# Two units' decay logarithms move behind the phase border, and the residual adds are queued together

## The chip, the cores and the metric

The kernel runs on one core of one Trainium2 chip. The metric is the device time of one launch in microseconds; the kernel before has a median of 293.94 us over 7 runs (291.76 to 295.33). Engine names follow the profile: PE is the matmul engine, ACT the activation engine, DVE the vector engine, POOL the one that also issues the DMAs which cast or accumulate, SP the one that issues plain loads, stores and transposes.

## What is computed

A linear recurrence with a complex decay for each channel, and then a gated feed-forward layer on its output:

```python
mag = np.sqrt(a_re * a_re + a_im * a_im)
scale = np.minimum(mag, 0.999) / (mag + 1e-06)
a_re_n, a_im_n = (a_re * scale, a_im * scale)
for t in range(S):                       # S = 768, B = 4, H = 8, D = 48
    new_re = ar * S_re - ai * S_im       # ar, ai: decay of step t
    new_im = ar * S_im + ai * S_re
    S_re, S_im = (new_re + k[t] v[t]^T, new_im)
    y[t] = q[t] @ S_re
...
ffn_out = (gelu(x @ w_gate) * (x @ w_val)) @ w_out      # x: y as 3072 x 384
out = x + sigmoid(x @ w_res) * ffn_out
```

The decay enters through the logarithm of its magnitude, 0.5 ln(re^2 + im^2), cut at ln 0.999, and its angle, arctan(im / re). Both are summed along time, and the sums turn the recurrence into products of scaled and rotated q and k.

## The kernel before

**Tiling.** A chunk `g` is 256 time steps of one batch with all 8 heads: two tiles (`C = 2`) of 128 rows and 384 columns, together 128x768. There are 12 chunks, ordered so that the four batches' first thirds come first. They are grouped into units: unit 0 is chunk 0, unit 1 chunks 1 and 2, unit 2 chunks 3 and 4, unit 3 chunks 5 and 6, up to unit 6 with chunk 11. Chunks 4 to 11 continue an earlier one (`NEXT`), so they need the state before them and its decay.

**Magnitude and angle of one chunk.** `squares(g)` forms the square of the real part (L213) and of the imaginary part (L224 on DVE for chunks 1 to 4, L227 on ACT otherwise) and adds them on DVE into the tile `lm` (L231). `p1_steps(g)` has three steps: `s0` takes the logarithm of `lm` in place and halves and cuts it on DVE (L239); `s1` and `s2` take a logarithm and an exponent of the real part, which gives its inverse, and multiply the imaginary part with it (L249). `p1_arctan` takes the arctangent. `cs_l` sums `lm` along time by matmuls (L267), and a later step takes E and its inverse Ei from them by exponents. `cs_t` does the same for the angles (L286, L288) and reduces them to one turn (L290, L291, L296); it writes its result over `lm`. `p2_sin` makes cosine and sine (the tile CS). `products` multiplies q by E and k by Ei (L349, L354) and by CS into the padded operands padQ and padK (L361), which from chunk 3 on SP transposes by DMA into QT and KT (L365).

**The decay of the state at a chunk's border** is a product of three factors in turned form, 96 partitions by 8 heads. `decay0(g)` makes the first: the exponent of row 0 of `lm` on ACT (1x384), a write of this row to a scratch line in DRAM, and `turn`, two reads of that line in turned order (L311) into the tile `m1`. `decay2` does the same for two rows of E and Ei. `multiply` forms the product on DVE (L342, L343); `enter_state` applies it to the state (L378) and rounds it (L380) for the attention matmuls.

**Order.** The program is written as a ramp (chunks 0 to 4) and then, for each unit u, `phase_x(u)` and `phase_y(u)`. `phase_y(u)` is the gate and value matmuls of unit u (`gv_step`: L575, L579, gelu, L582) with the first half of the next unit's attention and the squares of the unit two ahead; chunk 6 (`HELD`) has its squares in `phase_x(1)`. `phase_x(u)` has the logarithm and exponent work: for the next unit the cumulative sums, exponents and sines, for the unit after it the steps of `p1_steps`, beside the second half of unit u's attention and the output matmuls of unit u-1 (`op_step`, L599, L602). `weave` mixes such streams by written-out fractions of the phase. ACT changes its function table at the borders (L613), and `tab` fixes the order of these table loads and of the functions that need them, but not of copies and squares. A list scheduler then sets each engine's order by program order and by its own model of when an instruction is ready; each engine and each queue works its list in order.

**Queues.** SP has the loads of a, q and k, the output writes (L606) and the transposes. POOL has the loads of v and the weights, the turns, and for each output tile but the last unit's a residual add, an accumulating DMA of x onto the output (L608), which waits for that tile's L606. The output tile `ot` has two buffers, x has eight, `m1` three.

Of the kernel before, what the change touches and what calls it, by code (L numbers as in the profile page):

```python
# [28 lines left out]
def kernel(  # L29
# [34 lines left out]
    I2PI = 1.0 / (2.0 * math.pi)  # L64
    TURN = 3
    LATE0, LATE1 = 0.6, 1.0
    LNMAX = 0.5 * math.log(0.998001)


# [56 lines left out]
    psY = ctx.enter_context(tc.tile_pool(name="psY", bufs=1, space=PSUM))  # L126
    psD = ctx.enter_context(tc.tile_pool(name="psD", bufs=1, space=PSUM))

    T = {}
    order = mybir.DependencyInfo(mybir.DependencyClass.NoSync, mybir.DependencyReason.DATA)  # L130

    def tab(ins):
# [75 lines left out]
    def squares(g):  # L208

        def q0():  # L210
            T["lm", g] = pS.tile([128, W], FP, tag="s", name="lm")
            with paced("gelu"):
                nc.scalar.activation(out=T["lm", g], in_=flat(T["ar", g]), func=AF.Square)  # L213

        def q1():
            if g < 5:
                if g == 0:
                    T["sq"] = hb.tile([128, 4, 2, DM], FP, tag="h2", name="sq0")
                t = T["sq"][:, g % 4].rearrange("p a m -> p (a m)")
            else:  # L220
                t = pE.tile([128, W], FP, tag="E", name="sq")
            T["sq", g] = t
            if g in DVSQ:
                nc.vector.tensor_tensor(out=t, in0=flat(T["ai", g]), in1=flat(T["ai", g]), op=OP.mult)  # L224
            else:
                with paced("gelu"):
                    nc.scalar.activation(out=t, in_=flat(T["ai", g]), func=AF.Square)  # L227

        def q2():
            with paced("gmul"):  # L230
                nc.vector.tensor_tensor(out=T["lm", g], in0=T["lm", g], in1=T["sq", g], op=OP.add)  # L231
        return [q0, q1, q2]

    def p1_steps(g):
# [73 lines left out]
    def turn(nm, g, md, n):  # L308
        m = mp.tile([128, n, H], FP, tag=nm, name=nm)
        for u in range(2):  # L310
            nc.gpsimd.dma_start(out=m[u * D:(u + 1) * D].rearrange("p r h -> p (r h)"),  # L311
                                in_=md.rearrange("r (h d) -> d (r h)", h=H))
        T[nm, g] = m

    def decay0(g):
        if g not in NEXT.values():
            return
        e = T["s", g][0:1, 0:DM]
        act(out=e, in_=T["lm", g][0:1, 0:DM], func=AF.Exp)
        md = dr.tile([1, DM], FP, tag="d1", name="d1")  # L320
        nc.gpsimd.dma_start(out=md, in_=e)
        turn("m1", g, md, 1)

    def decay2(g):
        if g in NEXT.values():
# [13 lines left out]
    def multiply(g):  # L339
        m = T["m2", g]  # L340
        M = mp.tile([128, H], FP, tag="M", name="M")
        nc.vector.tensor_tensor(out=M[0:DD], in0=m[0:DD, 0], in1=m[0:DD, 1], op=OP.mult)  # L342
        nc.vector.tensor_tensor(out=M[0:DD], in0=M[0:DD], in1=T["m1", g][0:DD, 0], op=OP.mult)  # L343
        T["M", g] = M

    def products(g):
# [248 lines left out]
    def op_step(u, jj):  # L595
        h2 = T["h2", u]
        ps = psM.tile([128, DM], FP, tag="mm", padded_shape=[128, 512], name="op")
        for ffi in range(KF):
            nc.tensor.matmul(out=ps, lhsT=h2[:, ffi, jj * 128:(jj + 1) * 128], rhs=wo[:, ffi, :],  # L599
                             start=(ffi == 0), stop=(ffi == KF - 1))  # L600
        ot = ob.tile([128, DM], FP, tag="ot", name="ot")
        nc.vector.scalar_tensor_tensor(out=ot, in0=T["sg", u][:, jj], scalar=1.0, in1=ps, op0=OP.add, op1=OP.mult)  # L602
        t0 = (CHUNK[UNITS[u][0] + jj // C] * C + jj % C) * 128
        if u == NU - 1:
            nc.vector.tensor_tensor(out=ot, in0=ot, in1=T["x", token(u, jj)], op=OP.add)
        nc.sync.dma_start(out=out[t0:t0 + 128, :], in_=ot)  # L606
        if u < NU - 1:
            nc.gpsimd.dma_start(out=out[t0:t0 + 128, :], in_=T["x", token(u, jj)], accum_op=OP.add)  # L608


    def table(nm):
        def f():
# [6 lines left out]
    def token(u, jj):  # L619
        return UNITS[u][0] * C + jj  # L620
# [4 lines left out]
    def call(f, *a):  # L625
        return lambda: f(*a)
# [17 lines left out]
    def phase_x(u):  # L644

        pend = []
        g1 = gs(u + 1)
        p1g = [g for w in range(NU) if P1AT.get(w, w - 2) == u for g in gs(w)]
        now = [g for g in p1g if g in g1]
        ahead = [g for g in p1g if g not in g1]  # L650
        ops = [call(op_step, u - 1, jj) for jj in range(len(gs(u - 1)) * C)]
        att = att_steps(u, 1)
        if not g1:
            weave((0.0, 0.8, att), (0.1, 1.0, ops))
            return

        def csl(g, c):
            pend.append(cs_l(g, c))

        def ex():  # L660
            pend.pop(0)()

        def p1(g):
            return (squares(g) if g == HELD else []) + p1_steps(g) + [call(decay0, g)]
        csls = [call(csl, g, c) for g in g1 for c in range(C)]
        exs = [ex for _ in g1 for _ in range(C)]
        dec = [call(decay2, g) for g in g1]
        cst = [call(cs_t, g, c) for g in g1 for c in range(C)]
        sin = [call(p2_sin, g) for g in g1]
        table("natural_log_exp_and_others")()  # L670
        if now:
            atn = [table("trig_and_small")] + [call(p1_arctan, g) for g in now + ahead]
            pn = zip_steps([p1(g) for g in now])
            weave((0.0, 0.05, pn[:2]), (0.06, 0.1, csls), (0.12, 0.25, pn[2:]), (0.26, 0.4, exs),
                  (0.28, 0.48, zip_steps([p1(g) for g in ahead])),
                  (0.5, 0.5, dec), (0.55, 0.65, atn), (0.62, 0.8, cst), (0.9, 0.95, sin),
                  (0.0, 0.8, att), (0.0, 0.25, ops) if u == 1 else (0.1, 1.0, ops))
            return
        atn = [table("trig_and_small")] + [call(p1_arctan, g) for g in ahead]
        weave((0.0, 0.12, csls), (0.05, 0.5, zip_steps([p1(g) for g in ahead])), (0.12, 0.45, exs),  # L680
              (0.46, 0.46, dec), (0.2, 0.65, cst), (0.7, 0.95, atn + sin), (0.0, 0.8, att), (0.1, 1.0, ops))

    def ramp():

        g0, g1, g2 = gs(0) + gs(1)
        pend = {}

        def csl(g):
            pend[g] = [cs_l(g, c) for c in range(C)]

        def ex(g):
            for f in pend[g]:
                f()
            decay2(g)

        def cst(g):
            for c in range(C):
                cs_t(g, c)
        g3, g4 = gs(2)
        p = {g: p1_steps(g) for g in range(5)}  # L700
        q = {g: squares(g) for g in range(5)}
        pr = products(g0)

        def run(*fs):
            for f in fs:
                f()
        table("natural_log_exp_and_others")()
        run(*q[g0], p[g0][0], p[g0][1])
        csl(g0)
        run(p[g1][1], p[g0][2], q[g1][1], p[g1][2])  # L710
        ex(g0)
        run(p[g2][1], q[g2][1], p[g2][2])
        table("trig_and_small")()
        pr[0]()
        pr[2]()
        for g in (g0, g1, g2):
            if g > g0:
                T["f", g] = flat(T["ar", g])
            p1_arctan(g)
            cst(g)  # L720
            if g == g0:
                run(q[g1][0], q[g1][2], q[g2][0], q[g2][2])
        p2_sin(g0)
        pr[1]()
        pr[3]()
        a0 = attention_first(g0, 0, 0)
        table("natural_log_exp_and_others")()
        run(p[g1][0], p[g2][0])
        run(*a0[:2])
        csl(g1)  # L730
        csl(g2)
        run(*a0[2:4], *q[g3], p[g3][1], p[g3][2])
        ex(g1)
        run(*a0[4:7], *q[g4], p[g4][1])
        ex(g2)
        run(p[g4][2], p[g3][0], p[g4][0], call(decay0, g4), *a0[7:])
        with tc.issue_after(T["row"].ins):
            load_q(2, T["ld", "w", 2])
        table("trig_and_small")()
        p2_sin(g1)  # L740
        p2_sin(g2)
        with tc.issue_after(T["ld", "k", 2].ins):
            load_a(5)
        load_w_out()
        with tc.issue_after(T["ld", "ai", 5].ins):
            load_a(6)
        p1_arctan(g3)
        p1_arctan(g4)
# [34 lines left out]
    for u in range(NU + 1):  # L783
        if u > 0:
            phase_x(u)
        phase_y(u)
        for g in gs(u + 2):
            with paced("turn"):
                load_q(g)
            after_landing(T["k", g], call(load_v, g))  # L790
        while T["a"] < min(NG, gs(u + 1)[-1] + 7 if gs(u + 1) else NG):
            with paced("turn"):
                load_a(T["a"])
# [30 lines left out]
```

## Time and profile before

| | value |
|---|---|
| median of 7 runs | 293.94 us |
| the profiled execution | 294.86 us |
| its span in the trace | 293.1 us |
| granted PE clock, mean | 0.951 |
| POOL waiting for output writes at L608 | 54.1 us, 13 times |
| POOL waiting for row writes before a turn (L311), from a real part's row | 17.0 us, 3 times |
| residual adds | 22 of 192 KB, 4.3 us to landing (median) |
| ACT table loads | 21 of 1.28 us |

The span by stages, each bordered by the first gelu of a unit or the table load that ends its gelus (us busy in the stage, mean granted PE clock):

| stage | us | PE | DVE | ACT | clock |
|---|---|---|---|---|---|
| ramp | 0 to 52.3 | 26.7 | 37.7 | 40.1 | 0.87 |
| y(0) | 52.3 to 68.8 | 15.6 | 13.7 | 11.6 | 0.90 |
| x(1) | 68.8 to 90.6 | 16.1 | 19.8 | 20.1 | 0.99 |
| y(1) | 90.6 to 112.2 | 20.7 | 15.5 | 13.1 | 0.85 |
| x(2) | 112.2 to 132.8 | 19.7 | 17.5 | 18.3 | 1.00 |
| y(2) | 132.8 to 155.7 | 20.3 | 17.9 | 13.5 | 0.93 |
| the rest | 155.7 to 293.1 | 129.4 | 99.6 | 82.8 | 0.99 |

An idle time in a timeline stands in brackets with what ended it. An engine that waits is no loss by itself; it matters when what it does next is waited for.

### The profile page before, as it was taken

How to read it: one execution, taken by the hardware profiler on the slowest of the kernel's cores; microseconds unless marked ns; L12 is line 12 of the kernel's file. 1: busy time of each engine (PE TensorE's matmuls, PEld its weight loads, DVE VectorE, ACT ScalarE, POOL GpSimd, SP SyncE). 2: the span in 40 equal slices, each digit the busy share in tenths (PEclk: the TensorE clock that was granted, in tenths of full speed). 3: DMA queues.
4: the chain of work that ended last, by engine and by line, in shares of the span. 5: the costliest groups of instructions: out<-in, count | busy, mean ns of one | idle time of the engine just before them, and what ended most of it. 6: DMA issues, size and time to landing. Idle time of an engine off the chain costs nothing.

```text
span 293.1 us, 5128 instructions
## 1 busy us (share of the span) xinstructions
PE 248.4 (85%) x1834; PEld 149.3 (51%) x1848; DVE 221.6 (76%) x388; ACT 199.5 (68%) x333; POOL 95.6 (33%) x141
## 2 busy tenths in 40 slices
PE   0336956889876999999799999989999998999994
PEld 0123645777432456654366654555545665456782
DVE  0769997698997587989577999788977777564453
ACT  3886799679885489975659984779475655455250
POOL 4022933130445123567304482134911233100220
PEclk9999586799996899999889999999999999999999
DMA  9999999999999999999999869999499665910631
GB/s 148 187 175 187 154 199 195 172 173 199 166 182 191 136 186 182 161 170 142 193 209 178 94 118 193 199 184 83 75 210 204 99 58 112 192 29 5 158 55 54
DMA packets 176001, 44.01 MB, mean 150 GB/s; under 512 B 165092, under 2 KB 175976, under 8 KB 175976
## 3 DMA queue, kind: packets, MB, share of 16 engines
q1 hardware_dynamic: 140744, 33.05, 69.0%
q0 software_dynamic: 35232, 10.64, 35.7%
q8 instruction: 14, 0.23, 0.4%
q14 instruction: 11, 0.09, 0.1%
HBM read 31.33 MB, written 9.08 MB: 138 GB/s over the span
## 4 chain that ended last, share of the span: by engine, by line
PE 58%; ACT 17%; DVE 12%; DMA 6%; issue 4%; SPq 1%; DVEq 0%; ACTq 0%
PE gp L575 14%; PE vp L579 14%; PE op L599 11%; PE cst L286 4%; ACT L613 4%; DMA KT<-padK 3%; PE rp L591 3%; PE csl L267 2%; PE at L426 2%; ACT ar L140 2%; ACT CS L140 2%; PE dk L468 1%; DMA ai<-in_a_im_dram 1%; ACT E L140 1%; DVE ai L249 1%
## 5 line engine op out<-in xcount | busy, mean ns | idle before, releaser
L140 ACT ACTIVATE h<-gp 128x512 bf16<-128x512 f32 (+1 forms) x84 | 44.6, 536 | 44.4 <-PE gp L575 44.0
L582 DVE SCALAR_TENSOR_TENSOR h<-h,vp 128x512 bf16<-128x512 bf16 (+1 forms) x84 | 50.5, 608 | 24.7 <-PE vp L579 16.9
L575 PE MATMUL gp<-xT,wg 128*128 128x512 bf16 (+1 forms) x238 | 63.7, 364 | 2.7 <-ACT h L140 1.4
L579 PE MATMUL vp<-xT,wv 128*128 128x512 bf16 (+1 forms) x252 | 64.3, 363 | 0.2 <-ACT xT L564 0.2
L599 PE MATMUL op<-wo,h 128*128 128x384 bf16 x288 | 50.9, 326 | 1.4 <-ACT xT L564 0.8
L608 POOL DMA_DIRECT2D out_dram<-x x22 | 20.7, 973 | 54.1 <-DMA out_dram<-ot 54.1
L579 PEld LDWEIGHTS <-wv 128*128 128x128 bf16 x252 | 25.4, 101 | 23.7 <-issue 2.8
L599 PEld LDWEIGHTS <-h 128*128 128x128 bf16 x288 | 27.3, 98 | 18.8 <-issue 2.7
L575 PEld LDWEIGHTS <-wg 128*128 128x128 bf16 x252 | 24.6, 102 | 20.8 <-issue 4.6
L311 POOL DMA_DIRECT2D m<-d x32 | 23.9, 774 | 33.8 <-DMA d<-ar 17.0
L174 POOL DMA_DIRECT2D v<-in_v_dram x24 | 22.5, 942 | 18.8 <-DMA ai<-in_a_im_dram 11.7
L613 ACT ACT_TABLE_LOAD x21 | 26.9, 1283 | 1.1 <-PEq L808 0.7
L429 DVE TENSOR_TENSOR atm<-at,mask 128x512 bf16<-128x512 f32 x36 | 24.6, 683 | 4.0 <-PE at L426 4.0
L197 POOL COPY landed<-k 1x1 f32<-1x1 f32 x9 | 2.8, 308 | 59.4 <-DMA k<-in_k_dram 59.4
L267 PE MATMUL csl<-lm,lt0a 128*128 128x384 f32 x24 | 12.0, 584 | 10.5 <-DVE lm L239 10.5
L602 DVE SCALAR_TENSOR_TENSOR ot<-sg,op 128x384 f32<-128x384 f32 x24 | 13.2, 550 | 10.0 <-PE op L599 7.2
L286 PE MATMUL cst<-ai,ut0b 128*128 128x384 f32 x40 | 18.0, 538 | 0.3 <-ACT Ei L140 0.3
L140 ACT ACTIVATE ar<-ar 128x768 f32<-128x768 f32 x20 | 16.8, 851 | 0.0
L481 ACT CAST x<-y 128x384 bf16<-128x384 f32 x22 | 10.5, 478 | 9.2 <-PE y L478 8.8
L231 DVE TENSOR_TENSOR lm<-lm,sq 128x768 f32<-128x768 f32 x12 | 11.4, 950 | 7.0 <-ACT sq L227 6.8
L140 ACT ACTIVATE CS<-ai,hpi 128x768 bf16<-128x768 f32 x12 | 11.2, 932 | 7.8 <-DVE ai L296 7.8
L426 PE MATMUL at<-QT,KT 96*128 96x128 bf16 x144 | 14.3, 221 | 2.4 <-DMA KT<-padK 2.0
(112 smaller groups left out, 469.3 us busy)
## 6 DMA issues: line engine op xcount, KB each, us to landing
ar<-in_a_re_dram SPq DMA_DIRECT2D x24, 192.0 KB, 5.6
ai<-in_a_im_dram SPq DMA_DIRECT2D x24, 192.0 KB, 4.7
q<-in_q_dram SPq DMA_DIRECT2D x24, 192.0 KB, 5.0
k<-in_k_dram SPq DMA_DIRECT2D x24, 192.0 KB, 5.0
out_dram<-ot SPq DMA_DIRECT2D x24, 192.0 KB, 2.5
out_dram<-x POOLq DMA_DIRECT2D x22, 192.0 KB, 4.3
v<-in_v_dram POOLq DMA_DIRECT2D x24, 96.0 KB, 4.9
wg<-in_moe_w_gate_dram POOLq DMA_DIRECT2D x4, 288.0 KB, 8.0
```

The source lines that it names most:

```text
L140: return tab(nc.scalar.activation(**kw))
L174: held(nc.gpsimd.dma_start(out=t[:, c], in_=rows(v, g, c)), after)
L286: nc.tensor.matmul(out=cs, lhsT=tmat[c if s == 0 else 1], rhs=th[:, sl], start=True, stop=(s == 0 or c == 0))
L311: nc.gpsimd.dma_start(out=m[u * D:(u + 1) * D].rearrange("p r h -> p (r h)"), in_=md.rearrange("r (h d) -> d (r h)", h=H))
L426: nc.tensor.matmul(out=at[:, j], lhsT=T["KT", g][0:DD, x0 + j], rhs=T["QT", g][0:DD, x0 + j], start=True, stop=True)
L429: nc.vector.tensor_tensor(out=atm, in0=at, in1=mask4, op=OP.mult)
L575: nc.tensor.matmul(out=gp, lhsT=wg[:, fi, ffi * 128:(ffi + 1) * 128], rhs=xT[:, fi, :], start=(fi == 0), stop=(fi == KD - 1))
L579: nc.tensor.matmul(out=vp, lhsT=wv[:, fi, ffi * 128:(ffi + 1) * 128], rhs=xT[:, fi, :], start=(fi == 0), stop=(fi == KD - 1))
L582: T["gmul"] = nc.vector.scalar_tensor_tensor(out=h2[:, ffi, :], in0=h2[:, ffi, :], scalar=0.5, in1=vp, op0=OP.mult, op1=OP.mult)
L599: nc.tensor.matmul(out=ps, lhsT=h2[:, ffi, jj * 128:(jj + 1) * 128], rhs=wo[:, ffi, :], start=(ffi == 0), stop=(ffi == KF - 1))
L608: nc.gpsimd.dma_start(out=out[t0:t0 + 128, :], in_=T["x", token(u, jj)], accum_op=OP.add)
L613: tab(nc.scalar.preload_act_table_set(nm))
```

## The change

For chunks 3 to 6 the logarithm of the squared magnitude (`s0`) no longer stands in the ramp or a phase ahead: it opens the phase in which its sums are taken, `phase_x(1)` for chunks 3 and 4 and `phase_x(2)` for 5 and 6, ahead of the cumulative matmuls. Chunks 7 to 11 keep their logarithm where it was, so `phase_x(2)` has both pairs.

The first decay factor of chunks 4, 5 and 6 (chunk 3 has none) leaves as the raw squared row, right after the squares, or for chunk 6 after `phase_x(1)`; it is turned through DRAM as before, and its logarithm and a halved exponent are taken in turned form, 96x8. The cut at 0.999 for all chunks is made in `multiply`.

The residual adds are collected and queued after each `phase_x`. In the ramp's beginning chunk 0's steps and in its end the logarithms of chunks 3 and 4 are set in another order or left out.

```diff
+    LAZY = 2
+    LATER = UNITS[2] + UNITS[3]
+    MAGMAX = 0.999
...
                 nc.vector.tensor_tensor(out=T["lm", g], in0=T["lm", g], in1=T["sq", g], op=OP.add)
+            if g in LATER and g != HELD:
+                decay_raw(g)
...
-            nc.gpsimd.dma_start(out=m[u * D:(u + 1) * D].rearrange("p r h -> p (r h)"),
+            T["turned"] = nc.gpsimd.dma_start(out=m[u * D:(u + 1) * D].rearrange("p r h -> p (r h)"),
...
+    def decay_raw(g):
+        if g not in NEXT.values():
+            return
+        md = dr.tile([1, DM], FP, tag="d1", name="d1")
+        nc.gpsimd.dma_start(out=md, in_=T["lm", g][0:1, 0:DM])
+        turn("m1", g, md, 1)
+
+    def decay_exp(g):
+        if g not in NEXT.values():
+            return
+        m = T["m1", g][0:DD, 0]
+        act(out=m, in_=m, func=AF.Ln)
+        act(out=m, in_=m, func=AF.Exp, scale=0.5)
...
-        nc.vector.tensor_tensor(out=M[0:DD], in0=M[0:DD], in1=T["m1", g][0:DD, 0], op=OP.mult)
+        nc.vector.scalar_tensor_tensor(out=M[0:DD], in0=T["m1", g][0:DD, 0], scalar=MAGMAX, in1=M[0:DD],
+                                       op0=OP.min, op1=OP.mult)
...
-            nc.gpsimd.dma_start(out=out[t0:t0 + 128, :], in_=T["x", token(u, jj)], accum_op=OP.add)
+            T["acc"].append((t0, T["x", token(u, jj)]))
+    def residuals():
+        for t0, x in T["acc"]:
+            nc.gpsimd.dma_start(out=out[t0:t0 + 128, :], in_=x, accum_op=OP.add)
+        T["acc"] = []
...
         def p1(g):
-            return (squares(g) if g == HELD else []) + p1_steps(g) + [call(decay0, g)]
+            st = p1_steps(g)[1:] if u < LAZY else p1_steps(g) + [call(decay0, g)]
+            return (squares(g) if g == HELD else []) + st
+        lns = [f for g in g1 for f in (p1_steps(g)[0], call(decay_exp, g))] if u <= LAZY else []
...
-        weave((0.0, 0.12, csls), (0.05, 0.5, zip_steps([p1(g) for g in ahead])), (0.12, 0.45, exs),
+        weave((0.0, 0.1, lns), (0.06, 0.16, csls) if lns else (0.0, 0.12, csls), (0.05, 0.5, zip_steps([p1(g) for g in ahead])), (0.12, 0.45, exs),
...
-        run(*q[g0], p[g0][0], p[g0][1])
+        run(q[g0][0], p[g0][1], q[g0][1], q[g0][2], p[g0][2], p[g0][0])
         csl(g0)
-        run(p[g1][1], p[g0][2], q[g1][1], p[g1][2])
+        run(p[g1][1], q[g1][1], p[g1][2])
...
-        run(p[g4][2], p[g3][0], p[g4][0], call(decay0, g4), *a0[7:])
+        run(p[g4][2], *a0[7:])
...
             phase_x(u)
+        if u == 1:
+            with paced("turned"):
+                decay_raw(HELD)
+        residuals()
         phase_y(u)
```

More of the change, by code (lines that the diff above doesn't have):

```diff
@@ L127 @@
     psD = ctx.enter_context(tc.tile_pool(name="psD", bufs=1, space=PSUM))
-    T = {}
+    T = {"acc": []}
     order = mybir.DependencyInfo(mybir.DependencyClass.NoSync, mybir.DependencyReason.DATA)
```

## The prediction

> **What bounds the kernel now.** I read the page's engine shares and slices first, then the chain of waits over the stretches around the edit, then the timelines of ACT, DVE and SP there, and last the time from issue to landing of single transfers. I call the ramp 0 to 52.3 us, and then, with the first gelu as border, y(0) to 68.8, x(1) to 90.6, y(1) to 112.2, x(2) to 132.8, y(2) to 155.7; the rest is after that.
>
> ```profile
> PE 248.4 (85%) x1834; PEld 149.3 (51%) x1848; DVE 221.6 (76%) x388; ACT 199.5 (68%) x333; POOL 95.6 (33%) x141
> DMA  9999999999999999999999869999499665910631
> PE 58%; ACT 17%; DVE 12%; DMA 6%; issue 4%; SPq 1%; DVEq 0%; ACTq 0%
> ```
> Busy time, the DMA row of the 40 slices, and the chain by engine. PE carries 58% of the chain, and DMA is nine tenths or more busy for the first 22 slices (22 x 7.33 = 161 us): until there data may be as much the limit as any engine. After x(2) the chain is nearly all PE, which is busy 129.4 of the last 137.4 us. So what the change gains by about 155 us stays gained.
>
> ```profile
> 6.96 0.84 ACT L227 ACTIVATE sq<-ai 128x768 f32<-128x768 f32 x1 [1.26 <-DMA ai<-in_a_im_dram]
> 8.83 0.84 ACT L140 ACTIVATE lm<-lm 128x768 f32<-128x768 f32 x1 [1.02 <-DVE lm L231]
> 9.58 0.83 ACT L140 ACTIVATE ar<-ar 128x768 f32<-128x768 f32 x1
> ...
> 11.04 0.83 ACT L140 ACTIVATE ar<-ar 128x768 f32<-128x768 f32 x1
> ...
> 17.06 1.28 ACT L613 ACT_TABLE_LOAD   x1
> ...
> 42.55 0.48 ACT L549 CAST x<-y 128x384 bf16<-128x384 f32 x1 [0.49 <-PE y L544]
> 43.16 0.52 ACT L140 ACTIVATE ar<-lm 1x384 f32<-1x384 f32 x1
> 43.63 0.48 ACT L564 COPY xT<-tpx 128x384 bf16<-128x384 bf16 x1
> 44.12 1.28 ACT L613 ACT_TABLE_LOAD   x1
> ```
> ACT in the ramp: start, length, and in brackets the idle time before. From 8.83 to the table load at 17.06 nothing is idle, while ahead of 6.96 and of 8.83 ACT waits 1.26 and 1.02 us.
>
> ```profile
> 82.73 0.52 ACT L140 ACTIVATE ar<-lm 1x384 f32<-1x384 f32 x1 [0.80 <-DVE ai L249]
> 83.27 1.28 ACT L613 ACT_TABLE_LOAD   x1
> ...
> 126.74 0.55 DVE L291 TENSOR_TENSOR lm<-cst,lm 128x384 f32<-128x384 f32 x1
> 128.71 0.56 DVE L602 SCALAR_TENSOR_TENSOR ot<-sg,op 128x384 f32<-128x384 f32 x1 [1.42 <-DMA out_dram<-ot]
> 129.18 0.55 DVE L296 TENSOR_SCALAR ai<-lm 128x768 int32<-128x768 int32 x1
> ...
> 121.90 3.28 SPq L160 DMA_DIRECT2D ai<-in_a_im_dram  x2
> 125.28 4.34 SPq L606 DMA_DIRECT2D out_dram<-ot  x3
> ...
> 134.74 9.50 DMA KT<-padK
> ```
> The row exponent ahead of the table load that closes x(1); then DVE, SP and the chain in x(2) and y(2). SP issues loads until 125.2, the three output writes come behind them, and DVE stands 1.42 us at L602, whose tile waits for the first write. L296, the second sine pair and the gelu load follow. In y(2) PE waits for a transposed K that lands 9.50 us after its issue.
>
> **What the Trainium skill says.** "ScalarE: Activation LUTs", section What ACT_TABLE_LOAD costs: an ACTIVATE with immediate operands takes 186 ns + 0.833 ns an element, neighbours overlap by about 93 ns, and a table load is 1283 ns. The trace agrees: 768 elements would be 826 ns and take 0.83 to 0.84 us, the next one starts 0.73 us later, table loads are 1.28 us. For 96x8 this gives an estimate of 0.19 us, 0.10 net. The same page, section Table sets: the hidden batching unit, says that cheap functions such as copy are in every set; the trace has L444 copies under the logarithm table at 70.08. "DMA: Bandwidth & Descriptors", section Issuing engines are not separate DMA queues, says that transfers of SP and POOL run on the same 16 engines and interleave; the trace agrees: next to the residual add issued at 92.20 the transpose of 93.26 lands after 9.1 us, the one of 101.37, before the next add, after 6.0.
>
> **The change part by part.** Negative is earlier.
>
> 1. Ramp, start. The logarithm and the inverse (exponent) of chunk 0's real part leave the gap-free run: 2 x 0.73 = 1.46 us. They go into the holes of 1.26 and 1.02 us, each 0.84 long, so they are hidden; without these holes they would cost what they save. The L249 multiply (0.95) can now come before L239 on DVE and give back up to 0.3. Next late would be chunk 2's real part: SP issues its two halves from 7.47 on in 2.16 us, so the second at about 8.6, and 4.7 to landing gives 13.3; it is read at 14.73, so it just fits. Bounds -1.1 to -1.5; I take -1.4.
>
> 2. Ramp, end. Two logs (1.62 busy at 40.44), two L239 (1.01 at 42.11) and one row exponent (0.52) leave. They do not simply come off: the copy at 43.63 waits for PE, done at 43.59. But the table load was ordered behind the row exponent; now it can go where the logs were, and from 44.12 to the first gelu at 52.27 ACT is gap-free. Bounds 0 (it stays behind the copy) and -2.5; I take -1.3. Ramp: -2.7.
>
> 3. y(0). The squares of unit 3's first chunk sit between gelus. The imaginary part landed at 60.43 (POOL's wait for it ends there) and is read at 62.38, so this stretch can move by 1.95 at most, as DMA has no free slice before it. The new raw row of this chunk adds one row write and two turning reads on POOL, where it waits 13.02 us for k anyway (until 75.72): nothing. I cut the ramp's gain to -1.95.
>
> 4. x(1). Two logs and two L239 leave, two of each come in, now for unit 2 and at the head: nil in count. The cumulative matmuls, earlier done in y(0), come after them: table load ends 70.06, log 70.9, L239 71.4, matmul about 72.1, against E at 72.04 before: nothing. The two row exponents go (0.52 each, the second with 0.80 of idle), two small ACTIVATEs come (0.1 to 0.5 each, the dearer end from the 1x384 row). At the closing load this is 0.80 + 0.52 = 1.32. Bounds +0.5 (E later by a product) to -2.0; I take -1.3, so -3.25 at y(1).
>
> 5. Residual adds, y(1). For unit 0 they now come behind the raw row of the held chunk, whose turn waits for its row write (6.17 us at 102.32). The add of 92.20 thus goes to some 98 or later, off the K transpose of 93.26. That one landed at 102.36 and PE read it at 102.83, so without a faster transpose y(1) could gain only 0.5. With 9.1 falling to 6.0 it lands near 99.3, and PE would ask at 99.6. So -3.25 can pass; if the add stays, -0.5. POOL's other queue entries (v loads, decay turns) move forward at no price; the eight buffers of x hold units 0 and 1 and the first half of 2, just enough until then.
>
> 6. x(2). Here the logs of unit 3 are added to those of unit 4: 2 x 0.74 + 4 x 0.10 = +1.9 on ACT, +0.94 on DVE (two L239); the L343 scalar form costs the same 0.16. ACT was idle 0.21 + 0.32 + 1.69 = 2.2 us in this stretch, so the stretch alone grows between 0 and 1.9; I take +0.5. Behind the opening logs stand the cumulative matmuls and their four exponent pairs. SP's loads, fed by a full DMA, hardly move, so the first output write still lands at 128.6. If L602 keeps its place ahead of L296, all gain ends there; if L296 and the pads of chunk 5 are put ahead, as their earlier inputs allow, it passes. Bounds 0 and -2.75; I take -2.0.
>
> 7. y(2) and later. One add moves from 129.18 to beside the K transpose of 134.74, where two already run. Bounds -2.4 (all of PE's wait for it goes) and +3.0 (as much again as 9.1 against 6.0); I take 0. In the later pairs the output writes come as late as the adds can start (POOL waits for them 54.1 us in all), so their order changes little.
>
> Sum: -2.0 on the profiled execution, 294.86 us (span 293.1 and 1.76 around it), so 292.9. That execution is 0.9 above the median of 293.94; on the median the forecast is 291.9, or -0.7%.
>
> **The rivals.**
>
> R1, the gain is swallowed by the data stream. For it: the full DMA row, 0.47 us of slack at the K transpose, the DVE wait for the output write. Against it: the adds leave that transpose, and L296 need not stay behind L602. Then only about -0.4 remains: 293.5.
>
> R2, slower: x(2)'s opening. For it: 1.9 us on ACT and 0.94 on DVE before the exponent pairs, with PE busy 19.7 of 20.6 us there and DVE 17.5; and if L602 stands before more DVE work than L296 (two half-tile ops, 0.93), its wait ends at the same 128.7 with more behind it. Worth +1.9 - 0.4, with the add beside KT +1: about +2.4, 296.3. It decides once less than 0.5 us has been gained before 112 us. Against it: the ramp's saving is sure in kind.
>
> R3, more of the ramp comes through: the table load takes the whole 2.5 us of step 2, and the squares of step 3 are queued later between the gelus and don't bind. Then -1.4 - 2.5 - 1.3 + 0.5 and little lost behind, about -4: 289.9. Against it: the landing time of step 3. I count it into the forecast's side.
>
> **How the numbers follow.** Forecast with R3: 0.50; its own range 289.5 to 292.6. R1: 0.27, R2: 0.23. A run of this kernel tells no change from one within 0.5%, which is 1.47 us, so faster means under 292.47 and slower over 295.41. R1 is within, R2 above. The range leaves about one in ten on each side: 289.0 to 296.6.
>
> **What would show it.** Step 1: a log and an exponent in the two holes, table load near 15.6. Step 2: a table load near 41 with no log before it. Step 3: an ACT wait for the imaginary part near 60.4. Step 4: no 1x384 exponent before x(1)'s closing load. Step 5: the first KT landing after about 6 us. Step 6: L602 behind L296, or a longer wait at it. I am wrong if first gelus of y(1) come 3 us earlier and y(3)'s do not (then R1), or if x(2) lasts over 22 us (R2).

## The result, and the profile after

| | before | after |
|---|---|---|
| median | 292.84 us (64 runs, 290.87 to 296.08) | 290.14 us (27 runs, 288.33 to 293.68) |
| ratio | 1 | 0.9907, 95% interval 0.9888 to 0.9926 |
| the profiled execution | 294.86 us, span 293.1 | 293.38 us, span 291.6 |

The change makes the kernel 0.9% faster, 2.7 us. The 293.94 of the prediction is the median of the first 7 of the 64 executions. Every ratio here and below leaves out the executions that are over 1.5% above the fastest of their kernel (in e1, below, 5 of 17; with them its medians would give 0.995). The profile taken with the result belongs to one of the longest executions of the changed kernel, so a second profile of the same kernel stands beside it, called e1 (290.17 us, span 288.4): what both show is read as the change's, and what only one shows isn't.

The page after: engines, the DMA row of the 40 slices, the chain by engine and by line.

```profile
PE 245.3 (84%) x1834; PEld 147.9 (51%) x1848; DVE 221.4 (76%) x388; ACT 199.0 (68%) x336; POOL 95.6 (33%) x141
...
DMA  9999999999999999949999969999399765910631
...
PE 55%; DMA 15%; ACT 15%; DVE 8%; issue 4%; SPq 3%; DVEq 0%; ACTq 0%
PE op L619 13%; PE gp L595 11%; PE vp L599 11%; DMA KT<-padK 8%; DMA q<-in_q_dram 4%; PE csl L272 4%; PE cst L291 4%; DMA ar<-in_a_re_dram 3%; ACT L639 3%; PE at L446 2%; PE rp L611 2%; ACT lm L143 2%; PE cst L293 2%; SPq L385 1%; PE tpx L580 1%
```

The work is the same; ACT and DVE are as busy as before. DMA's share of the chain is 15% here where it was 6%, and more than half of it is a transposed K (8%). In e1 it is 6% again, with 2% for the K, so the larger share belongs to this execution and not to the change.

The start of the ramp on ACT, after:

```profile
7.33 0.83 ACT L230 ACTIVATE sq<-ai 128x768 f32<-128x768 f32 x1
9.18 0.84 ACT L143 ACTIVATE lm<-lm 128x768 f32<-128x768 f32 x1 [1.02 <-DVE lm L234]
...
12.63 0.87 ACT L143 ACTIVATE E<-csl 128x384 f32<-128x384 f32 x2 [0.41 <-PE csl L272]
13.91 0.87 ACT L143 ACTIVATE E<-csl 128x384 f32<-128x384 f32 x2 [0.41 <-PE csl L272]
...
17.00 1.28 ACT L639 ACT_TABLE_LOAD   x1
```

The first hole of before (1.26 us, ahead of 6.96) is filled, by two functions instead of one, so that the square of the imaginary part starts 0.37 later. The second hole is still there, and two new ones of 0.41 have come ahead of E. The table load has not moved: 17.00 against 17.06.

The end of the ramp on ACT, after:

```profile
38.33 2.05 ACT L541 COPY qk<-tp 96x512 bf16<-96x512 bf16 x4
40.39 1.28 ACT L639 ACT_TABLE_LOAD   x1
...
46.07 1.57 ACT L143 ACTIVATE ai<-ai 128x768 f32<-128x768 f32 x2
47.66 1.28 ACT L639 ACT_TABLE_LOAD   x1
```

The load of the sine's table went from 44.12 to 40.39, and the first gelu's from 50.97 to 47.66: 3.3 us. Then y(0), where ACT takes the squares of chunk 5 between the gelus:

```profile
59.00 0.84 ACT L216 ACTIVATE lm<-ar 128x768 f32<-128x768 f32 x1 [1.28 <-DMA ar<-in_a_re_dram]
...
61.59 0.84 ACT L230 ACTIVATE sq<-ai 128x768 f32<-128x768 f32 x1 [1.09 <-DMA ai<-in_a_im_dram]
```

Before, ACT waited for neither. Now both wait for their data, 2.4 us together (2.3 in e1).

How the rest goes is read from the ends of the stages. The table sets the two profiles of the changed kernel and those of all experiments side by side; every row comes from the ACT timeline (the table loads bound the stages), the landing times of the transposes and the windows. "K2" and "K3" are the first K transposes of units 2 and 3, in y(1) and y(2); "wait" is what PE waits for that stage's K, "clock" the mean granted clock in the stage.

| kernel | gelu of y(0) | gelu of y(1) | K2 issued, taking | landed | y(1): length, wait, clock | x(2) | K3 taking | y(2): length, wait | log of x(3) |
|---|---|---|---|---|---|---|---|---|---|
| before | 50.97 | 89.27 | 93.26, 9.1 | 102.4 | 22.9, 0, 0.85 | 19.3 | 9.5 | 24.2, 2.0 | 155.65 |
| after | 47.66 | 87.61 | 93.15, 7.2 | 100.4 | 23.5, 1.9, 0.93 | 19.8 | 9.0 | 22.7, 2.1 | 153.51 |
| e1, the same | 47.77 | 88.73 | 93.05, 7.3 | 100.4 | 21.2, 0.8, 1.00 | 19.7 | 7.1 | 21.3, 0.7 | 150.97 |
| e2 logs alone | 48.19 | 86.44 | 93.94, 7.0 | 100.9 | 26.5, 3.7, 0.87 | 19.8 | 5.6 | 20.4, 0 | 153.11 |
| e3 adds alone | 52.17 | 91.74 | 94.52, 7.1 | 101.6 | 21.7, 0, 0.92 | 18.0 | 8.4 | 21.6, 0.3 | 153.04 |
| e4 start alone | 51.09 | 89.49 | 93.31, 9.1 | 102.4 | 22.2, 0.7, 0.92 | 19.7 | 7.9 | 20.7, 0.1 | 152.02 |
| e5 one unit | 47.80 | 89.17 | 94.17, 6.3 | 100.5 | 22.5, 0, 0.85 | 18.9 | 9.0 | 21.9, 1.3 | 152.40 |
| e6 start mended | 47.26 | 85.57 | 91.55, 6.5 | 98.1 | 21.7, 1.7, 1.00 | 21.1 | 9.2 | 23.0, 2.4 | 151.36 |
| e7 squares later | 48.31 | 88.26 | 94.43, 8.1 | 102.5 | 23.6, 1.8, 0.93 | 20.0 | 6.8 | 21.2, 0.6 | 153.00 |
| e8 no adds | 47.84 | 88.57 | 92.62, 7.6 | 100.2 | 20.9, 0.8, 1.00 | 19.7 | 4.4 | 20.4, 0 | 149.57 |
| e9 raw row later | 48.84 | 86.76 | 93.67, 7.8 | 101.5 | 25.5, 2.3, 0.87 | 19.9 | 5.9 | 20.7, 0.2 | 152.85 |
| e10 adds held | 47.39 | 87.41 | 93.41, 7.3 | 100.7 | 22.6, 2.5, 1.00 | 19.8 | 4.7 | 20.4, 0 | 150.20 |
| e11 e6, e9, e10 in one | 46.35 | 88.84 | 94.06, 7.7 | 101.8 | 22.2, 2.2, 1.00 | 19.7 | 4.6 | 20.4, 0 | 151.22 |
| e12 more adds held | 47.18 | 88.72 | 93.08, 7.5 | 100.6 | 21.3, 1.0, 1.00 | 19.7 | 4.5 | 20.4, 0 | 150.13 |

After the last column every one of these profiles takes 137.4 to 138.9 us more, so nearly all is decided by then. Three readings:

1. y(1) is an account. PE is busy 18.6 to 18.7 us in it at clock 1.00, and 21.2 to 21.7 at 0.85 to 0.87. Take from the length what PE waits for K and what it is busy beyond 18.6, and 19.9 to 20.3 are left in every row (before: 22.9 - 2.6; e1: 21.2 - 0.8 - 0.1; e2: 26.5 - 3.7 - 2.9; after: 23.5 - 1.9 - 1.5). The start of y(1) varies by 6 us and K2's issue by only 3, because it stands in SP's queue behind the loads and output writes. So an earlier y(1) mostly becomes a longer wait: the earliest start but one, e2 at 86.44, has the longest; only e6, at 85.57, gets away with 1.7.

2. y(2) is simpler: 20.4 us of PE, plus the wait for K, within 0.9 us; in before, where PE was busy 21.6 us at a clock of 0.93, it is 1.8. It goes with the length of K3's transpose: at 5.6 us or less it is 20.4 in all five rows, at 9.0 and above 21.9 to 24.2.

3. In x(2) the rows without doubled logarithms (before, e3, e4, e5) have 18.0 to 19.7, mean 19.0; those with them 19.7 to 21.1, mean 19.9. The ranges touch, with one profile to a row, so this difference is an estimate.

Stage y(1) in before, and then in e1, from the windows: its length, then busy time of PE, PEld, DVE, ACT, POOL, the clock, DMA share and GB/s.

```profile
89.27:112.18 22.91, 21.19 (x137) 10.73 (x140) 16.81 (x29) 14.35 (x26) 6.22 (x9) 0.85 1.16 172
```

```profile
88.73:109.94 21.21, 18.70 (x139) 9.89 (x139) 17.54 (x30) 14.38 (x26) 7.07 (x11) 1.00 1.32 195
```

The same groups of matmuls, 137 and 139 of them in the records, keep PE busy for 21.2 us in the first and 18.7 in the second. That is the clock. A single pair of profiles thus shows differences in this stretch that belong to the execution and not to the edit; this is why the ratios below decide, and the profiles only say where.

### The profile page after: what moved, and what is told of

It is laid out like the page before. It is cut to its first block, busy times and chain, and to the rows that moved or that the text cites. A ratio compares the mean times of both kernels' runs of the same rounds, so it can differ in the third digit from the quotient of the medians.

```text
span 291.6 us, 5139 instructions
## 1 busy us (share of the span) xinstructions
PE 245.3 (84%) x1834; PEld 147.9 (51%) x1848; DVE 221.4 (76%) x388; ACT 199.0 (68%) x336; POOL 95.6 (33%) x141
## 4 chain that ended last, share of the span: by engine, by line
PE 55%; DMA 15%; ACT 15%; DVE 8%; issue 4%; SPq 3%; DVEq 0%; ACTq 0%
PE op L619 13%; PE gp L595 11%; PE vp L599 11%; DMA KT<-padK 8%; DMA q<-in_q_dram 4%; PE csl L272 4%; PE cst L291 4%; DMA ar<-in_a_re_dram 3%; ACT L639 3%; PE at L446 2%; PE rp L611 2%; ACT lm L143 2%; PE cst L293 2%; SPq L385 1%; PE tpx L580 1%
## 5 line engine op out<-in xcount | busy, mean ns | idle before, releaser
L602 DVE SCALAR_TENSOR_TENSOR h<-h,vp 128x512 bf16<-128x512 bf16 (+1 forms) x84 | 50.6, 608 | 23.9 <-PE vp L599 15.4
L599 PE MATMUL vp<-xT,wv 128*128 128x512 bf16 (+1 forms) x252 | 62.1, 354 | 1.2 <-ACT sg L143 1.2
L595 PE MATMUL gp<-xT,wg 128*128 128x512 bf16 (+1 forms) x238 | 61.4, 354 | 1.7 <-ACT h L143 1.0
L634 POOL DMA_DIRECT2D out_dram<-x x22 | 21.8, 1016 | 47.3 <-DMA out_dram<-ot 47.0
L619 PEld LDWEIGHTS <-h 128*128 128x128 bf16 x288 | 27.4, 98 | 19.3 <-issue 2.9
L595 PEld LDWEIGHTS <-wg 128*128 128x128 bf16 x252 | 23.8, 99 | 18.3 <-issue 1.6
L177 POOL DMA_DIRECT2D v<-in_v_dram x24 | 22.9, 959 | 17.7 <-DMA ai<-in_a_im_dram 11.7
L272 PE MATMUL csl<-lm,lt0a 128*128 128x384 f32 x24 | 13.3, 644 | 11.2 <-DVE lm L244 11.2
L622 DVE SCALAR_TENSOR_TENSOR ot<-sg,op 128x384 f32<-128x384 f32 x24 | 13.2, 549 | 8.4 <-PE op L619 6.9
L291 PE MATMUL cst<-ai,ut0b 128*128 128x384 f32 x40 | 17.1, 521 | 0.6 <-DVE ot L622 0.5
L446 PEld LDWEIGHTS <-KT 96*128 96x128 bf16 x144 | 10.3, 99 | 11.2 <-DMA KT<-padK 5.7
```

The source lines that it names most:

```text
L177: held(nc.gpsimd.dma_start(out=t[:, c], in_=rows(v, g, c)), after)
L272: nc.tensor.matmul(out=cs, lhsT=lmat[c], rhs=T["lm", g][:, sl], start=True, stop=True)
L291: nc.tensor.matmul(out=cs, lhsT=tmat[c if s == 0 else 1], rhs=th[:, sl], start=True, stop=(s == 0 or c == 0))
L446: nc.tensor.matmul(out=at[:, j], lhsT=T["KT", g][0:DD, x0 + j], rhs=T["QT", g][0:DD, x0 + j], start=True, stop=True)
L595: nc.tensor.matmul(out=gp, lhsT=wg[:, fi, ffi * 128:(ffi + 1) * 128], rhs=xT[:, fi, :], start=(fi == 0), stop=(fi == KD - 1))
L599: nc.tensor.matmul(out=vp, lhsT=wv[:, fi, ffi * 128:(ffi + 1) * 128], rhs=xT[:, fi, :], start=(fi == 0), stop=(fi == KD - 1))
```

## The experiments

All ratios are to the kernel before in the same comparison, with 95% intervals.

**e1: the change as it is, once more,** for a second profile and as the measure of the others.

> The changed kernel once more, for a profile beside the parts on one chip. All theories: ratio 0.991 to before. In the profile: the gelu table load that opens y(0) about 2.5 us earlier, the table load into the arctangents without logs ahead of it near 40.4 us, no gain at 17 us.

Measured: 0.9903 (0.9867 to 0.9939), the same as 0.9907. The table load near the start is again at 16.98, K2 takes 7.3.

**e2, e3, e4: the three parts alone.** e2 has the late logarithms with the raw rows, and leaves the order of chunk 0's steps and the residual adds as before. e3 has only the collected adds. e4 has only the other order of chunk 0's steps:

```diff
-        run(*q[g0], p[g0][0], p[g0][1])
+        run(q[g0][0], p[g0][1], q[g0][1], q[g0][2], p[g0][2], p[g0][0])
         csl(g0)
-        run(p[g1][1], p[g0][2], q[g1][1], p[g1][2])
+        run(p[g1][1], q[g1][1], p[g1][2])
```

> The late logs and raw decay rows alone; the order at the start and the residual adds stay as before. Theory A (the logs carry the whole gain, by the table load that moves up in the ramp and the row exponents that go): 0.991, 290.2 us. Theory B (the adds carry it, the logs only give back in x(2) what they gain): 1.000. Theory C (the start's order gives 1.4 us, the logs the rest): 0.995.

> The collected residual adds alone. On POOL this moves a single add past three other DMAs, all else keeps its order. Theory A: 1.000 within 0.3%. Theory B: 0.991, with the first K transpose landing after about 6 us where it took 9.1. Theory C: 1.000.

> The new order of chunk 0's first steps alone. Theory A: 1.000 within 0.3%, as the first cumulative matmul waits for DVE behind the L249 multiply, so that the table load stays near 17.0 us. Theory B: 1.000. Theory C: 0.995, with that table load near 15.6.

Measured: e2 0.9935 (0.9910 to 0.9961), e3 0.9956 (0.9935 to 0.9977), e4 0.9989 (0.9966 to 1.0013). The logarithms and the adds each carry a part that can be told from nothing; the new start carries none. The product is 0.9880 against 0.9907 of the whole, so the parts are not more than additive, and within their intervals they may be just that. So neither theory A (all in the logarithms) nor B (all in the adds) holds. What e3 gains is not shown in one place. In POOL's order only the first add of unit 0 moves, behind two turning reads and a factor's write, and it still goes ahead of K2 (92.25); the second goes at 99.47 instead of 103.61, as the turn ahead of it does, K2 takes 7.1 where before had 9.1, and PE waits 0.3 in y(2) where before waited 2.0.

**e5: late logarithms for unit 2 alone.** Chunks 5 and 6 take theirs where they did before, in x(1), so the doubled logarithms stand there and x(2) has none.

```diff
-    LAZY = 2
-    LATER = UNITS[2] + UNITS[3]
+    LAZY = 1
+    LATER = UNITS[2]
...
-        if u == 1:
-            with paced("turned"):
-                decay_raw(HELD)
```

> The change with late logs for unit 2 only: chunks 5 and 6 get their logs and row exponents in x(1) as before, so x(2) has no doubled logs; start and collected adds as in the change. Theory D (x(2)'s two extra logs hide behind the data stream): ratio to before 0.9905, the change's own. Theory F (they cost their 1.9 us on ACT): 0.984. If unit 3's freed row exponents in x(1) matter: 0.995.

Measured: 0.9966 (0.9943 to 0.9989). x(2) is back at 18.9, but x(1) takes 21.8 us from its log load to y(1)'s gelu load, against 19.5 in e1 and 20.5 before. Somewhere the logarithms of two units stand in one phase: in x(1), with the row exponents of chunks 5 and 6, that costs 2.3 us against e1, and in x(2) 0.9 (reading 3).

**e6: the start mended.** Step 1 of the prediction had failed, and the trace gave two candidates: the exponent that slipped ahead of the square of the imaginary part, and the L254 multiply that DVE now does ahead of the cut. Here both are put behind (the split of the step in two is left out below).

```diff
-            act(out=T["s", g], in_=T["s", g], func=AF.Exp, scale=-1.0)
-            nc.vector.tensor_tensor(out=T["th", g], in0=T["s", g], in1=T["th", g], op=OP.mult)
+            with tc.issue_after(T["sqi", g].ins) if g == 0 else nullcontext():
+                act(out=T["s", g], in_=T["s", g], func=AF.Exp, scale=-1.0)
...
+            with tc.issue_after(T["cut", g].ins) if g == 0 else nullcontext():
+                nc.vector.tensor_tensor(out=T["th", g], in0=T["s", g], in1=T["th", g], op=OP.mult)
```

> The change with chunk 0's exponent held behind the square of the imaginary part and its multiply held behind the cut on DVE, so that the first cumulative matmul starts near 10.3 us again. The table load at 17.0 us comes 0.9 earlier. Theory D (loads swallow what the ramp gains): ratio to before 0.9905, with the two ACT waits for the loads of chunk 5 in y(0) longer by what is gained, 2.4 to 3.3 us together. Theory G (each us of the ramp comes through): 0.987.

DVE around 10 us, first in e1 (the change), then in e6:

```profile
9.45 0.95 DVE L254 TENSOR_TENSOR ai<-ar,ai 128x768 f32<-128x768 f32 x1
10.32 0.56 DVE L244 TENSOR_SCALAR lm<-lm 128x768 f32<-128x768 f32 x1
```

```profile
9.79 0.56 DVE L244 TENSOR_SCALAR lm<-lm 128x768 f32<-128x768 f32 x1 [0.50 <-ACT lm L143]
10.26 0.95 DVE L258 TENSOR_TENSOR ai<-ar,ai 128x768 f32<-128x768 f32 x1
```

Measured: the table load comes at 16.45, 0.53 earlier; the ratio is 0.9903 (0.9867 to 0.9940), as e1's. The cut was in the way, as the order on DVE says: ACT is kept by the matmul sums behind it (0.41 ahead of E). The other 0.9 us of step 1 don't come even so, since E still waits for PE. And what comes is not seen at the end: e6 starts y(1) at 85.57, earliest of all, and pays with waits for K of 1.7 and 2.4 us.

**e7: chunk 5's squares later.** If the two waits for chunk 5's data in y(0) take the gain, queueing these squares later between the gelus should give it back.

```diff
-        weave((0.0, 1.0, gv), *pr, (0.55, 0.56, dec3), (0.5, 0.95, sq), ...
+        weave((0.0, 1.0, gv), *pr, (0.55, 0.56, dec3), (0.6, 1.0, sq) if u == 0 else (0.5, 0.95, sq), ...
```

> The change with chunk 5's squares put later among the gelus of y(0), past the landing of its loads. Theory D: the two ACT waits (1.28 and 1.09 us) go, y(0) ends up to 2 us earlier, and PE waits for the first transposed K in y(1) instead, so the ratio to before stays 0.9905. Theory G: 0.985.

Measured: 1.0008 (0.9981 to 1.0034), the whole gain lost. The waits in y(0) do shrink, to 0.86 and 0.34 (2.34 in e1), and y(0) ends at 67.09, but x(1) grows to 21.2 (19.5 in e1). Further on, the first residual add is again ahead of K2 on POOL (93.23 and 94.43), K2 takes 8.1 and lands at 102.5. The row of chunk 5, which follows its squares, has moved on POOL too (see e9). These go together here, so the run doesn't say which of them costs more. It does say that these waits are no loss that one can simply take out.

**e8: no residual adds for all units but the last,** to bound what they cost in any place. The output then lacks x there.

> The change with the residual adds of units 0 to 5 left out, so that the output lacks x there: 22 transfers fewer. Theory D (the adds slow the transposes and the loads): ratio to before 0.975 to 0.983, K transposes of unit 2 and 3 landing after about 6 us, where they took 7.2 and 9.0. Theory H (the adds run in free DMA time): 0.9905.

The issues between 133 and 137 us with the time from issue to landing, first after, then e8:

```profile
out_dram<-x POOLq DMA_DIRECT2D x2, 192.0 KB, 8.3
...
KT<-padK SPq DMA_TRANSPOSE x1, 9.0
```

```profile
KT<-padK SPq DMA_TRANSPOSE x1, 4.4
QT<-padQ SPq DMA_TRANSPOSE x1, 4.4
```

Measured: 0.9869 (0.9837 to 0.9901). K3 falls from 9.0 to 4.4, and y(2) to its 20.4. K2 does not fall: 7.6, against 7.2 and 7.3 with the adds. Why K2 stays that long is not shown. Loads are not its neighbours: in e8 SP issues none between 86.3 and 101.5, and those ahead land some 5 us after their issue, so by about 92, before K2 is issued at 92.62. For about 1 us of its flight the engines move 11 GB/s or less. In y(2) the adds are what K3 meets.

**e9: chunk 5's raw row later.** In the change this row is written at 78.61, and its turn keeps POOL until 84.12; behind it stand two v loads (L177) and, further on, the first add. This is POOL after:

```profile
78.61 0.53 POOL L333 DMA_DIRECT2D d<-lm  x1
84.12 1.29 POOL L316 DMA_DIRECT2D m<-d  x2 [4.98 <-DMA d<-lm]
...
85.77 1.79 POOL L177 DMA_DIRECT2D v<-in_v_dram  x2
...
95.78 0.50 POOL L333 DMA_DIRECT2D d<-lm  x1
96.27 0.96 POOL L634 DMA_DIRECT2D out_dram<-x  x1
96.87 0.87 POOL L300 DMA_DIRECT2D row<-lm  x1
100.85 1.31 POOL L316 DMA_DIRECT2D m<-d  x2 [3.11 <-DMA d<-lm]
102.15 0.98 POOL L634 DMA_DIRECT2D out_dram<-x  x1
```

The first add goes at 96.27 behind other turns and the write of chunk 6's row (95.78), and the second waits for that row's turn at 100.85. e9 sends the row together with chunk 6's:

```diff
-            if g in LATER and g != HELD:
+            if g in LATER and g not in UNITS[3]:
...
-                decay_raw(HELD)
+                for g in UNITS[3]:
+                    decay_raw(g)
```

> The change with chunk 5's raw row sent after x(1), next to chunk 6's, so that POOL does not stand 5 us in x(1) for this row's turn and the second decay factor of chunk 4 leaves earlier. Only three entries of POOL's order move. Theory J (the wait of DVE for that factor, 2.0 and 1.5 us at 100 us in the two profiles, is on the path): ratio to before 0.985. Theory D (PE waits for the first transposed K until the same time anyway): 0.9905, with DVE's wait gone and PE's kept.

POOL in e9:

```profile
80.81 1.76 POOL L177 DMA_DIRECT2D v<-in_v_dram  x2
...
89.89 0.98 POOL L333 DMA_DIRECT2D d<-lm  x2
92.89 0.94 POOL L634 DMA_DIRECT2D out_dram<-x  x1 [2.03 <-DMA out_dram<-ot]
...
94.00 2.88 POOL L316 DMA_DIRECT2D m<-d  x4
96.54 1.31 POOL L634 DMA_DIRECT2D out_dram<-x  x1
```

Measured: 0.9977 (0.9951 to 1.0004), so three quarters of the gain go with three entries in POOL's queue. The first add is ahead of K2 again, K2 takes 7.8 and lands at 101.5, and PE waits 2.3 us for it. A part of the long y(1), 25.5 us, is the clock of 0.87 in this profile. The direction is as the prediction's step 5 has it; how much of the 0.74% between e1 and e9 is K2, the profiles don't settle. DVE's wait for the factor (2.03 us in after, 1.49 in e1) is gone in e9, and the kernel is slower all the same, so theory J has fallen.

The add has a rival that is not tested. In e9 the v loads go 5 us earlier as well. In after, e1, e6, e8, e10 and e12 the turn of chunk 5's row stands ahead of both these loads, and the ratios are 0.9869 to 0.9907. In e2 it stands ahead of one of them, in e3, e4, e5, e7, e9 and e11 ahead of none, and the ratios are 0.9919 to 1.0008. No run has the loads late with an add ahead of K2, or early without one.

**e10: unit 1's adds held back** until K3 has landed; nothing but POOL's order differs from the change.

```diff
-            nc.gpsimd.dma_start(out=out[t0:t0 + 128, :], in_=x, accum_op=OP.add)
+            held(nc.gpsimd.dma_start(out=out[t0:t0 + 128, :], in_=x, accum_op=OP.add), after)
...
+        if u == 2:
+            pr.append((0.45, 0.45, [lambda: residuals(T["turn", "K", UNITS[3][0]])]))
...
-        residuals()
+        if u != 2:
+            residuals()
```

> The change with unit 1's four residual adds held until the first K transpose of unit 3 has landed. Only POOL's order moves. Theory D (a transpose beside adds lands 3 us later and PE waits for it): that transpose lands after 5 to 6 us where it took 9.0 and 7.1, PE's wait near 143 goes, ratio to before 0.986. Theory H (the later adds only move the traffic onto the next transposes and loads): 0.9905.

POOL in e10:

```profile
132.75 0.51 POOL L300 DMA_DIRECT2D row<-lm  x1
139.77 3.62 POOL L634 DMA_DIRECT2D out_dram<-x  x4 [6.50 <-DMA KT<-padK]
```

And in e10 the issues between 133 and 137 us:

```profile
KT<-padK SPq DMA_TRANSPOSE x1, 4.7
```

Measured: 0.9871 (0.9827 to 0.9914), median 289.36. K3 takes 4.7, y(2) the bare 20.4, and all the adds still fit in later: as good as having no adds at all. It beats the changed kernel by 0.36% on the middle values, but the intervals overlap (0.9827 to 0.9914 and 0.9888 to 0.9926): what is shown is the stage, not yet the kernel's time.

**e11: e6, e9 and e10 in one.**

> The start order mended, the raw row later and the adds held, all in one. If each keeps its gain: ratio to before 0.982. If the data stream swallows them: 0.9905.

Measured: 0.9919 (0.9887 to 0.9951), no better than the change. The start is early (gelu of y(0) at 46.35), y(2) is bare, but with chunk 5's row away the first add goes at 93.09, K2 lands at 101.8 and PE waits 2.2. On the middle values the raw row in its place, which looks like a block, was worth more than the two gains; the intervals of e10 and e11 overlap.

**e12: e10, and unit 0's adds held** until K2 has landed.

> The change with the residual adds of unit 1 held until the first K transpose of unit 3 has landed (as in e10), and those of unit 0 held in the same way until the first K transpose of unit 2 has landed; on POOL's queue only, nothing else is moved. Theory D (an add that runs beside a K transpose delays it, at unit 2 as at unit 3): K of unit 2 lands some 6 us after its issue instead of 7.3, PE's wait of 2.47 us near 100 falls under 1.5, ratio to the kernel before about 0.983. Theory H (nothing further: the held adds run beside the V and product transposes that follow, and PE's wait near 100 is not theirs): K of unit 2 still over 7 us, ratio as e10's, about 0.987.

Measured: 0.9873 (0.9825 to 0.9921), as e10. K2 takes 7.5 with no add near it, against 7.3 in e10 with one 3.4 us behind it. PE's wait in y(1) is 1.0 and not 2.5, but y(1) also begins 1.3 us later, so that is the account of reading 1 and no gain. Nothing here speaks for moving unit 0's adds further; the ratio alone, from six executions, doesn't exclude the 0.983 of theory D.

## Why the prediction was right

The forecast was -2.0 us (-0.7%), measured are -2.7 us (-0.9%, 0.7 to 1.1). Rival R2 didn't come. R3's 289.9 nearly did (290.14), with one of its two reasons: step 2 came in full, but the squares of step 3 did wait for their data. The sum was right with several terms wrong against each other, so that it came this close is in part luck.

**Step 1, wrong.** -1.4 was taken, 0 came (17.00 against 17.06), and e4 alone is 0.9989. Over all profiles this load comes at 17.06 to 17.56 in the old order (before, e2, e3) and at 16.98 to 17.56 in the new one, so 0.3 on average at most. The step priced the log and the exponent as filling one hole each. Both went into the first, which pushed the square 0.37 back. The L249 multiply came ahead of the cut, which the step had named at up to 0.3; behind that the two sums on PE bound ACT, which it had not seen. It counted ACT's time and took the inputs of its later work for given.

**Step 2, mis-sized.** -1.3 was taken with -2.5 as bound; 3.3 us came at the gelu's load though step 1 gave nothing. The table load near 41, named as the sign, came (40.39). From the two ACT timelines the 3.3 add up as 1.6 for the two logs, 0.5 for the row exponent, 0.5 for the wait of the cast at 42.55, which now lies beside the cosines, 0.6 for a copy (L444, at 50.39) that now comes behind the gelu load, and 0.2 from further ahead. The first three make the bound, nearly; the step took half of it out of caution, and had not seen the copy. That copy now stands ahead of the first gelu, so at the gelu itself, the prediction's border of the ramp, 2.5 came (49.81 against 52.27): the whole bound.

**Step 3, right in the place, wrong in a term put at nothing.** The cap of 1.95 was named with its place, and ACT's waits for chunk 5 came there (after 1.28 and 1.09, e1 0.74 and 1.60). The end of y(0) moved by -1.2 in after (67.62 against 68.78); in e1 by +0.5. The cap took the landing at 60.43 as given; here ACT has the data at 61.59 and 61.69, while in e2, e6 and e9 y(0) ends 2.4 to 2.7 earlier than before, more than the cap allows. The term put at nothing is chunk 5's raw row, "where it waits 13.02 us for k anyway". It comes behind that wait, at 78.61, its turn waits another 4.98 on POOL, and e9, which moves it away, loses three quarters of the gain.

**Step 4, over-sized.** x(1) is 0.5 to 1.0 us shorter (20.0 and 19.5, from 20.5), where 1.3 was taken: the row exponents went, and the logs at the head took some back. So y(1) starts 1.7 (after) or 0.5 (e1) earlier and not 3.25.

**Step 5, right in where, wrong in the cause and the size.** It said that y(1) hangs on the landing of K2, that the add moves behind it, and that K2 would take 6.0 and land at 99.3 with PE asking at 99.6. K2 lands at 100.4 (102.4 before), and in e1 PE asks at 99.6. PE waits for K in after and in e1:

```profile
100.40 0.40 PE L446 MATMUL at<-QT,KT 96*128 96x128 bf16 x4 [1.94 <-DMA KT<-padK]
143.78 0.40 PE L446 MATMUL at<-QT,KT 96*128 96x128 bf16 x4 [2.12 <-DMA KT<-padK]
```

```profile
100.41 0.40 PE L446 MATMUL at<-QT,KT 96*128 96x128 bf16 x4 [0.83 <-DMA KT<-padK]
141.24 0.40 PE L446 MATMUL at<-QT,KT 96*128 96x128 bf16 x4 [0.71 <-DMA KT<-padK]
```

The landing 2.0 us earlier is the part of the gain that both profiles share. But what moves the add is not what the step names, the held chunk's row and its turn: the add goes at 96.27 ahead of that turn (100.85), and e9 has that row too and its add goes at 92.89. Chunk 5's row and the collecting do it together: e2 has the row without the collecting (93.17), e3 the collecting without the row (92.25). That the add left K2 as forecast is luck. Over all rows the mechanism is also weaker than the step has it. With the add issued 0.8 to 1.2 us ahead of K2 (before, e2, e4, e7, e9, e11) K2 takes 7.0 to 9.1, mean 8.1; with no add ahead of it on POOL, and none until 2.1 us after its issue (after, e1, e6, e8, e10, e12), 6.5 to 7.6, mean 7.2. That is 0.9 us from the add, not 3.1: the 6.0 of another transpose at 101.37 was no measure for this one, as it had an add behind it itself (103.61) and q loads (103.49). The Trainium skill's page "DMA: Bandwidth & Descriptors", section Issuing engines are not separate DMA queues, has transfers of all issuers interleave on the same engines; K3 agrees, with 9.0 beside the adds and 4.4 without (e8). That doesn't explain K2's 7.6 in e8, with no add at all. And the add's place isn't all: in e5 and e3, with the add 1.6 and 2.3 us ahead, K2 took 6.3 and 7.1. With these two counted as adds ahead, 0.5 us is left between the means, and the ranges overlap.

**Step 6, right in sign, under-sized.** +0.5 was taken for x(2); by reading 3 it is about +0.9. On ACT in e1 the stretch opens like this:

```profile
109.94 1.28 ACT L639 ACT_TABLE_LOAD   x1
111.23 0.84 ACT L143 ACTIVATE lm<-lm 128x768 f32<-128x768 f32 x1
111.98 0.43 ACT L143 ACTIVATE m<-m 96x8 f32<-96x8 f32 x2
112.32 1.56 ACT L143 ACTIVATE lm<-lm 128x768 f32<-128x768 f32 x2
113.78 0.19 ACT L143 ACTIVATE m<-m 96x8 f32<-96x8 f32 x1
```

The small ones cost as worked out (two in 0.43, one 0.19), four logarithms stand ahead of the first E at 115.09, and ACT has hardly a hole left in this phase, where 2.2 us of them were counted as cover. The order of L602 was guessed rightly: on DVE in e1 it stands behind the second L296 (L622 and L301 here) and no longer waits (1.42 before). The wait isn't the order's alone, though: e3 keeps the old order, and its L602 waits for nothing either.

```profile
127.40 0.56 DVE L301 TENSOR_SCALAR ai<-lm 128x768 int32<-128x768 int32 x1
127.86 0.56 DVE L622 SCALAR_TENSOR_TENSOR ot<-sg,op 128x384 f32<-128x384 f32 x1
```

**Step 7, right that it is open.** 0 was taken between -2.4 and +3.0. K3 took 9.0 and 7.1 beside the adds, 4.4 to 4.7 where none is near (e8, e10, e11, e12), and PE's wait went from 2.0 to 2.1 and 0.7. The change itself is near nothing here; what was missed is that the adds could have been taken away from K3 altogether, which e10 does.

**R1** spoke of the same place as step 5: it is where e2 and e9 lose what the ramp gave. e2, without collected adds, starts y(1) 2.8 us earlier than before and ends it 0.8 later (112.96 against 112.18). That is R1's mechanism, though a part of it is the clock of 0.87 there. The change ends y(1) 1.1 us earlier than before (e1 2.2); that the adds' new place does this is argued, not shown: 0.9935 and 0.9907 are not clear of each other.

Left open: why e3's one moved add is worth 0.4%, how much of e7's and e9's loss is K2 and how much the v loads, and what makes K2 long where no add is near.

## What to carry to other kernels

A gain on an engine ends at the next thing that waits for data, so follow it to the first transfer whose issue stands in a queue, and ask what that transfer will share the DMA engines with; here the 3.3 us of the ramp came to 1.9 us (0.65%) in e2, and moving three entries of a DMA queue lost three quarters of the whole gain in e9. Price such an entry by what stands behind it in its queue, even where the queue seems to wait anyway. Bulk transfers that nobody waits for can go behind those that somebody does: tying four of them to the landing of K3 cost nothing that e10 shows and brought the stage to its bare PE time; for K2, in e12, it brought nothing. A gap-free run on one engine isn't shortened by what leaves it until the inputs of the rest have been followed too.

## What was unexpected of the hardware

The granted PE clock in y(1) was 0.85 to 1.00 from profile to profile, which is 18.6 to 21.7 us of PE for the same work. Over whole executions its mean was 0.957 for the kernel before (140 executions) and 0.964 to 0.969 for after, e1, e2, e6, e8, e10 and e12, but 0.956 to 0.961 for e3, e4, e5, e7, e9 and e11. The first seven are those in which the turn of chunk 5's row stands ahead of at least one of the v loads of e9's account; why that should go with the clock, no run tells. In the kernel before, clock and time don't go together (correlation 0.05); in e2 they do (-0.66). The clock alone is not the gain: among executions at 0.9605 or more, e1's ten average 290.05 us and the 23 of the kernel before in the same comparison 292.91. Below that, where e1 has only two, it is 291.61 against 293.00.

Transposed Ks of the same size took very different times. K3 took 4.4 to 4.7 us with no add near it and 5.6 to 9.5 beside adds; K2 took 6.3 to 9.1, and 7.6 with no add and no load beside it.
